# The opening of a retention and two-MLP kernel: a load moved by one place, the state's products ahead of y, and a first in-projection in three passes

## The chip, the cores and the metric

The kernel runs on one core of a Trainium2 chip. The metric is the device time of one execution in microseconds (us). Before the change it is 607.47 us, the median of three runs. One further execution was profiled; all rows below come from its trace.

## The reference

Three stages follow one another on 1,536 tokens (2 batches of 768) with 512 features.

```python
# 1. retention, 8 heads of 64, state carried along the 768 positions of a batch
state = gamma * state + outer(k[t], v[t])
y[t]  = scale * q[t] @ state
# 2. MLP, 512 -> 2048 -> 512
h = x @ w_in
x = (h * sigmoid(1.702 * h)) @ w_out
# 3. RMS norm, then a gated MLP, 512 -> 1536 -> 512
xn  = x / sqrt(mean(x * x) + 1e-6) * rms_g
out = (silu(xn @ w_gate) * (xn @ w_val)) @ w_out2
```

The weights of both MLPs come as float64. The kernel turns them into float32 itself.

## The kernel before

**Retention in chunks.** The sequence is cut into chunks of 128 positions, 6 to a batch. For chunk c the kernel loads two tiles of 512 KB: qk (queries and keys, `load_qk`) and kv (keys and values with positions on the partitions, `load_kv`). GpSimd scales them to qd and kd (`prep`, L225 and L232). TensorE forms the scores (`score_products`, L252), VectorE multiplies them by the decay masks (`masks`, L264), and TensorE sums y in PSUM from two parts: `inter` (L281: the state of the chunk before, times qd) and `intra` (L294: masked scores times values). `update_products` (L333: kd times values) gives the chunk's addition to the state. ScalarE decays the old state (`decay`, L341), VectorE adds (`add_update`, L349). y becomes x, split in two float32r tiles that sum to it: ScalarE writes the high part (`x_high`, L310), VectorE the low part (`x_low`, L316).

**Weights.** `load_next` (L138) loads one half of a weight block, 512 KB of float64, into one of 4 buffers; `queue` sets their order: first half of block 0, first half of block 1, second half of block 0, and so on. `convert_next` makes it float32: two ScalarE operations (L165, L166), then three of VectorE (`convert_rest`, L171, L172, L174). With `split=True` it issues the two of ScalarE and returns the rest, to be issued later. Without it, it also issues one more load at the end. A converted half is then split again into float32r high and low tiles (`split_in` for the first MLP's input weights, tiles wih and wil; `split_out` for its output weights, woh and wol): ScalarE L369, VectorE L370.

**First MLP.** A block of 512 tokens (4 chunks) goes through 128 hidden features at a time, a step. `in_proj` sums 12 products in one PSUM bank: for each of 4 slices of the 512 features, high by high, high by low and low by high (L364 to L366). Then ScalarE's gelu (L396) and its high part gh (L398), VectorE's low part gl (L399), and 12 products per step that accumulate the output (acc).

**Order.** The code around the change is the opening: chunks 0 to 3, which make up the first token block, the first conversions, and `prep(4)`. Its order on TensorE, VectorE, ScalarE and GpSimd is the order in which it is written, since `in_order` chains each instruction to the one before on its engine. Loads go through one queue of SP in the order written. After the opening a planner orders the work by the order of the code and by when it expects inputs to be ready; the first two steps are held behind the last instruction of the opening on each engine. Step 0 issues two conversions, the splits for its output and for step 2's input, then its in-projection and gelu; the accumulation of step 0 is issued in step 1, with the decay and state of chunk 4.

Of the kernel before, what the change touches and what calls it, by code (L numbers as in the profile page):

```python
# [23 lines left out]
KD = DM // 128  # L24
# [25 lines left out]
def tile_retention_mlp_swiglu(  # L50
# [19 lines left out]
    nc = tc.nc  # L70
# [12 lines left out]
    ps_t = pool("ps_t", 2, space=PSUM)  # L83
# [20 lines left out]
    def psum(p, name):  # L104
        return p.tile([128, T], F32, tag=p.name, name=name)
# [27 lines left out]
    def load_next():  # L133
        n = count["loaded"]
        if n < len(queue):
            kind, i, half = queue[n]
            t = st_p.tile([128, 512], U64, tag="st", name=f"{kind}{i}{half}_64")
            nc.sync.dma_start(out=t, in_=sources[kind][i][:, half * 512:half * 512 + 512])  # L138
            words[queue[n]] = t
            count["loaded"] += 1  # L140

    def convert_next(split=False):
        n = count["converted"]
        if n < len(queue):
            rest = convert(*queue[n])
            count["converted"] += 1
            if split:
                return rest
            rest()
            load_next()  # L150

    def convert(kind, i, half):

        if kind == "w1" and half == 0:
            raw[kind, i] = wr_p.tile([128, 1024], U32, tag="wr", name=f"{kind}{i}")  # L160
        o = slice(half * 512, half * 512 + 512)
        w = words.pop((kind, i, half)).bitcast(U32).rearrange("p (n two) -> p n two", two=2)
        low, high = w[:, :, 0], w[:, :, 1]
        q, t = tmp(f"q{kind}{i}{half}"), tmp(f"u{kind}{i}{half}").bitcast(U32)
        nc.scalar.activation(out=q, in_=high.bitcast(F32), func=ACTF.Copy, scale=2.0 ** -112)  # L165
        nc.scalar.activation(out=t, in_=low, func=ACTF.Copy, scale=2.0 ** -29)  # L166
        m = q.bitcast(U32)
        return lambda: convert_rest(kind, i, half, o, high, q, m, t)
# [17 lines left out]
    parts = {}  # L186
# [20 lines left out]
    xt = {}  # L207

    def load_qk(c):
        p, tag = (wr_p, "wr") if c < CPB else (ld_p, "ld")  # L210
        t = p.tile([128, 2, NP, C], F32, tag=tag, name=f"qk{c}")
        nc.sync.dma_start(out=t.rearrange("p a n c -> p (a n c)"), in_=qk[c])
        ld["qk", c] = t

    def load_kv(c):
        p, tag = (wr_p, "wr") if c < CPB else (ld_p, "ld")
        t = p.tile([128, 2, H, D], F32, tag=tag, name=f"kv{c}")
        nc.sync.dma_start(out=t.rearrange("p a h d -> p (a h d)"), in_=kv[c])
        ld["kv", c] = t
# [3 lines left out]
    def prep_q(c):  # L223
        t = tmp(f"qd{c}")
        nc.gpsimd.tensor_tensor(  # L225
            out=t.rearrange("p (n c) -> p n c", n=NP), in0=ld["qk", c][:, 0], in1=qd_sb, op=ALU.mult
        )
        at["qd", c] = t

    def prep_k(c):  # L230
        t = tmp(f"kd{c}")
        nc.gpsimd.tensor_tensor(  # L232
            out=t.rearrange("p (h d) -> p h d", h=H),
            in0=ld["kv", c][:, 0],
            in1=sm_sb[:, 0:H].to_broadcast([128, H, D]),
            op=ALU.mult,
        )
        at["kd", c] = t

    def prep(c):  # L240

        if c % NC:
            prep_q(c)
        if c % NC < NC - 1:
            prep_k(c)

    def score_products(c, p):
        t = ld["qk", c]
        sc = at["sc", c] = [psum(p, f"sc{c}_{e}") for e in range(2)]
        for n in range(NP):  # L250
            for e in range(2):
                nc.tensor.matmul(  # L252
                    out=sc[e][:, n * C:(n + 1) * C],
                    lhsT=t[64 * e:64 * e + 64, 1, n, :],
                    rhs=t[64 * e:64 * e + 64, 0, n, :],
                    start=True,
                    stop=True,
                )
# [14 lines left out]
    def inter(c, p):  # L273
        y = at["y", c] = psum(p, f"y{c}")
        if c % NC == 0:
            return
        qd = at.pop(("qd", c))
        for n in range(NP):
            for e in range(2):
                r = slice(64 * e, 64 * e + 64)  # L280
                nc.tensor.matmul(  # L281
                    out=y[r, n * C:(n + 1) * C],
                    lhsT=S_two[(c - 1) % 2][r, n, :],
                    rhs=qd[r, n * C:(n + 1) * C],
                    start=(n == 0),
                    stop=False,
                    skip_group_check=True,
                )

    def intra(c):  # L290
        y = at["y", c]
        for n in range(NP):
            for e in range(2):
                nc.tensor.matmul(  # L294
                    out=y[64 * e:64 * e + 64, n * C:(n + 1) * C],
                    lhsT=ld["kv", c][:, 1, 2 * n + e, :],
                    rhs=at["a", c, e][:, n * C:(n + 1) * C],
                    start=(c % NC == 0 and n == 0),
                    stop=True,
                    skip_group_check=True,  # L300
                )

    def x_of(c):
        j, i = divmod(c, CPB)
        if j not in xt:
            xt[j] = [xt_p.tile([128, KD, T], F32R, tag=f"xt{min(j, 1)}{s}", name=f"xt{j}{s}") for s in "hl"]
        return [x[:, :, i * C:(i + 1) * C] for x in xt[j]]

    def x_high(c):
        nc.scalar.activation(  # L310
            out=x_of(c)[0], in_=at["y", c].rearrange("p (n c) -> p n c", n=NP), func=ACTF.Copy
        )

    def x_low(c):
        xh, xl = x_of(c)
        nc.vector.tensor_tensor(  # L316
            out=xl, in0=at.pop(("y", c)).rearrange("p (n c) -> p n c", n=NP), in1=xh.bitcast(F32), op=ALU.subtract
        )
# [7 lines left out]
    def update_products(c, p):  # L326
        u = at["u", c] = psum(p, f"u{c}")
        kd = at.pop(("kd", c))
        vt = ld["kv", c][:, 1].rearrange("p h d -> p (h d)")
        for n in range(NP):  # L330
            for e in range(2):
                h = slice((2 * n + e) * D, (2 * n + e) * D + D)
                nc.tensor.matmul(  # L333
                    out=u[64 * e:64 * e + 64, n * D:(n + 1) * D], lhsT=kd[:, h], rhs=vt[:, h], start=True, stop=True
                )

    def decay(c):
        if c % NC:
            S_old, S_sb = S_two[(c - 1) % 2], S_two[c % 2]
            for n in range(NP):  # L340
                nc.scalar.activation(  # L341
                    out=S_sb[:, n, :], in_=S_old[:, n, :], func=ACTF.Copy, scale=sm_sb[:, H + n, :]
                )

    def add_update(c):
        u3 = at.pop(("u", c))[:, 0:NP * D].rearrange("p (n d) -> p n d", n=NP)
        S_sb = S_two[c % 2]
        if c % NC:
            nc.vector.tensor_tensor(out=S_sb, in0=u3, in1=S_sb, op=ALU.add)  # L349
        else:  # L350
            nc.vector.tensor_copy(out=S_sb, in_=u3)
# [9 lines left out]
    def product(out, a, b, first, last):  # L361

        (ah, al), (bh, bl) = a, b
        nc.tensor.matmul(out=out, lhsT=ah, rhs=bh, start=first, stop=False)  # L364
        nc.tensor.matmul(out=out, lhsT=ah, rhs=bl, start=False, stop=False)  # L365
        nc.tensor.matmul(out=out, lhsT=al, rhs=bh, start=False, stop=last)  # L366
# [10 lines left out]
        halves(hi, lo, g)  # L377
        return hi, lo

    def in_proj(ps, w, x):  # L380
        for k in range(KD):
            product(ps, [t[:, k * 128:(k + 1) * 128] for t in w], [t[:, k, :] for t in x], k == 0, k == KD - 1)


    gt = {}
# [2 lines left out]
    def mlp1_in(i):  # L388
        j, f, _, _ = STEPS[i]
        ps = psum(ps_h, f"h{j}_{f}")  # L390
        in_proj(ps, parts.pop(("wi", i)), xt[j])
        return ps

    def mlp1_act(i, ps):
# [347 lines left out]
    nc.sync.dma_start(out=qd_sb.rearrange("p n c -> p (n c)"), in_=qdec)  # L742
    load_kv(1)
    load_qk(2)
    load_next()
    load_kv(2)
    load_qk(3)
    load_kv(3)
    for _ in range(3):
# [26 lines left out]
    x_high(1)  # L776
    add_update(1)
    x_low(1)
    rest = convert_next(split=True)
    decay(2)  # L780

    score_products(2, ps_a)
    masks(2)
    inter(2, ps_h)
    score_products(3, ps_a)
    rest()
    intra(2)
    update_products(2, ps_t)
    prep(3)
    masks(3)  # L790
    x_high(2)
    add_update(2)
    x_low(2)
    split_in(0)
    rest = convert_next(split=True)
    decay(3)
    inter(3, ps_h)
    intra(3)
    update_products(3, ps_t)
    rest()  # L800
    x_high(3)
    x_low(3)
    add_update(3)
    load_next()
    load_next()
    split_in(1)
    prep(4)
    ends = in_order(opening)
# [16 lines left out]
    for i, (j, f, first, last) in enumerate(STEPS):  # L825
# [5 lines left out]
        k = min(i, len(STEPS) - 5)  # L831
# [5 lines left out]
        ps = mlp1_in(i)  # L837
# [76 lines left out]
    for g in range(0, F2, 2):  # L914
# [7 lines left out]
        n = len(work) - 10  # L922
# [31 lines left out]
    for g in range(0, JOIN, 2):  # L954
        reload("w2", g)
        reload("w2", g + 1)
        w = [set_tasks(k, g) for k in ("wg", "wv")]
# [96 lines left out]
```

## Time and profile before

| | us |
|---|---|
| median of 3 runs | 607.47 (606.02 to 608.62) |
| profiled execution: device time | 605.8 |
| profiled execution: span of the trace | 604.0 |
| TensorE matmul busy | 591.9 (98%) |
| VectorE busy | 443.1 (73%) |
| ScalarE busy | 365.0 (60%) |
| GpSimd busy | 28.1 (5%) |

The span is that of the trace; the device time holds a little more. A matmul's busy time overlaps that of the next, because matmuls are pipelined; so TensorE's share says that it seldom waits, not that it is at its peak. The granted TensorE clock is full in all 40 slices of the span.

### The profile page before, as it was taken

To read this page: it belongs to the slowest core of one execution; us is meant where nothing else is said; L and a number is where in the kernel's file an instruction comes from. 1 tells how busy PE (TensorE), PEld (TensorE's weight loads), DVE (VectorE), ACT (ScalarE), POOL (GpSimd) and SP (SyncE) were. 2 spreads that over 40 slices of the span, in tenths; PEclk is the share of its full clock that TensorE was granted. 3 is DMA by queue.
4 is the path that set the end of the run, shared out by engine and by line. 5 is a ranking of instruction groups with operands and counts; after the bars stand their busy time and mean duration, and the time that the engine had idled before them with its cause. 6 is when DMAs were issued, how large, how long until landed. Compare 5 with 4: busy or idle time off the path is not lost.

```text
span 604.0 us, 9246 instructions
## 1 busy us (share of the span) xinstructions
PE 591.9 (98%) x3354; PEld 492.8 (82%) x3354; DVE 443.1 (73%) x793; ACT 365.0 (60%) x691; POOL 28.1 (5%) x28
## 2 busy tenths in 40 slices
PE   7899999999999999999999999999999999999997
PEld 5677878888888878888887788898988889988885
DVE  3899988777797868989977999664655756655542
ACT  3577767766666658877757876453444536544532
POOL 3502200000112000000000000000000000000000
PEclk9999999999999999999999999999999999999999
DMA  8876744434678545337523423130221376643521
GB/s 337 343 232 239 245 157 139 126 122 144 187 220 244 160 139 163 105 95 235 159 105 97 128 107 124 69 112 30 98 77 65 110 247 219 228 144 105 174 71 69
DMA packets 32877, 93.14 MB, mean 154 GB/s; under 512 B 3904, under 2 KB 4160, under 8 KB 32832
## 3 DMA queue, kind: packets, MB, share of 16 engines
q1 hardware_dynamic: 32400, 92.42, 47.4%
q8 instruction: 26, 0.43, 0.3%
q10 hardware_dynamic: 432, 0.14, 0.1%
q14 instruction: 19, 0.16, 0.1%
HBM read 73.67 MB, written 18.87 MB: 153 GB/s over the span
## 4 chain that ended last, share of the span: by engine, by line
PE 85%; DVE 7%; DMA 3%; ACT 3%; issue 2%; ACTq 0%; SPq 0%; DVEq 0%
PE acc L364 6%; PE acc L365 6%; PE h L365 6%; PE acc L366 6%; PE h L364 6%; PE h L366 6%; PE o L364 5%; PE o L365 5%; PE o L366 5%; DMA qk<-in_qk 2%; DVE qw L172 1%; DVE wil L370 1%; DVE w L174 1%; DVE qw L171 1%; PE sc L252 1%
## 5 line engine op out<-in xcount | busy, mean ns | idle before, releaser
L364 PE MATMUL acc<-gh,woh 128*128 128x512 f32 x192 | 76.2, 399 | 0.9 <-ACT gh L398 0.9
L365 PE MATMUL acc<-gl,woh 128*128 128x512 f32 x192 | 75.2, 391 | 0.7 <-DVE gl L399 0.7
L366 PE MATMUL acc<-gh,wol 128*128 128x512 f32 x192 | 74.9, 390 | 0.0
L369 ACT ACTIVATE wih<-w 128x512 fp32r<-128x512 f32 x48 | 30.2, 631 | 53.5 <-PE h L365 51.5
L365 PE MATMUL o<-w3l,gh 128*128 128x512 f32 x144 | 56.3, 391 | 0.0
L364 PE MATMUL o<-w3h,gh 128*128 128x512 f32 x144 | 56.1, 391 | 0.0
L366 PE MATMUL o<-w3h,gl 128*128 128x512 f32 x144 | 56.1, 390 | 0.0
L370 DVE TENSOR_TENSOR wil<-w,wih 128x512 fp32r<-128x512 f32 x48 | 34.7, 726 | 22.3 <-ACT wih L369 22.2
L172 DVE CUSTOM_DVE_ANT_0 qw<-qw,uw 128x1024 uint16<-128x1024 uint16 x68 | 49.6, 730 | 0.8
L165 ACT ACTIVATE qw<-w 128x512 f32<-128x512 f32 x68 | 45.3, 666 | 1.0 <-DMA w<-in_w 1.0
L166 ACT ACTIVATE uw<-w 128x512 uint32<-128x512 uint32 x68 | 45.5, 670 | 0.0
L364 PEld LDWEIGHTS acc<-gh,woh 128*128 128x128 f32 x192 | 36.0, 188 | 9.7 <-ACT gh L398 1.2
L365 PEld LDWEIGHTS acc<-gl,woh 128*128 128x128 f32 x192 | 36.1, 188 | 8.5 <-DVE gl L399 1.6
L366 PEld LDWEIGHTS acc<-gh,wol 128*128 128x128 f32 x192 | 36.1, 188 | 7.5
L369 ACT ACTIVATE woh<-w 128x512 fp32r<-128x512 f32 x48 | 30.2, 630 | 16.6 <-DVE w L174 10.7
L171 DVE TENSOR_SCALAR qw<-qw 128x512 uint32<-128x512 uint32 x68 | 30.4, 448 | 10.5 <-ACT qw L165 10.5
L370 DVE TENSOR_TENSOR wol<-w,woh 128x512 fp32r<-128x512 f32 x48 | 32.9, 686 | 4.6 <-ACT woh L369 4.6
L370 DVE TENSOR_TENSOR gl<-gw,gh 128x512 fp32r<-128x512 f32 x24 | 16.6, 692 | 26.8 <-ACT gh L369 26.7
L399 DVE SCALAR_TENSOR_TENSOR gl<-g,gh 128x512 fp32r<-128x512 f32 x48 | 33.1, 689 | 3.1 <-ACT gh L398 1.4
L369 ACT ACTIVATE gh<-gw 128x512 fp32r<-128x512 f32 x24 | 15.1, 631 | 28.5 <-PE o L365 24.5
L366 PEld LDWEIGHTS o<-w3h,gl 128*128 128x128 f32 x144 | 27.0, 188 | 5.5
L364 PEld LDWEIGHTS o<-w3h,gh 128*128 128x128 f32 x144 | 27.1, 188 | 4.8 <-ACT w3h L369 0.2
(1115 smaller groups left out, 1509.1 us busy)
## 6 DMA issues: line engine op xcount, KB each, us to landing
w<-in_w SPq DMA_DIRECT2D x68, 512.0 KB, 4.7
qk<-in_qk SPq DMA_DIRECT2D x12, 512.0 KB, 6.8
kv<-in_kv SPq DMA_DIRECT2D x12, 512.0 KB, 6.7
g0d<-gs SPq DMA_DIRECT2D x12, 256.0 KB, 2.2
g2d<-gl SPq DMA_DIRECT2D x12, 256.0 KB, 2.1
gw<-g0d SPq DMA_DIRECT2D x12, 256.0 KB, 2.8
gw<-g2d SPq DMA_DIRECT2D x12, 256.0 KB, 2.7
out<-o SPq DMA_DIRECT2D x11, 256.0 KB, 2.4
```

Of the source, the lines that this page charges most:

```text
L165: nc.scalar.activation(out=q, in_=high.bitcast(F32), func=ACTF.Copy, scale=2.0 ** -112)
L166: nc.scalar.activation(out=t, in_=low, func=ACTF.Copy, scale=2.0 ** -29)
L171: nc.vector.tensor_scalar(out=m, in0=m, scalar1=3, scalar2=None, op0=ALU.logical_shift_left)
L172: nc.vector.tensor_tensor(out=m, in0=m, in1=t, op=ALU.add)
L174: nc.vector.scalar_tensor_tensor(out=dst, in0=high, scalar=0x80000000, in1=m, op0=ALU.bitwise_and, op1=ALU.bitwise_or)
L252: nc.tensor.matmul(out=sc[e][:, n * C:(n + 1) * C], lhsT=t[64 * e:64 * e + 64, 1, n, :], rhs=t[64 * e:64 * e + 64, 0, n, :], start=True, s ...
L364: nc.tensor.matmul(out=out, lhsT=ah, rhs=bh, start=first, stop=False)
L365: nc.tensor.matmul(out=out, lhsT=ah, rhs=bl, start=False, stop=False)
L366: nc.tensor.matmul(out=out, lhsT=al, rhs=bh, start=False, stop=last)
L369: nc.scalar.activation(out=hi, in_=src, func=ACTF.Copy)
L370: nc.vector.tensor_tensor(out=lo, in0=src, in1=hi.bitcast(F32), op=ALU.subtract)
L399: nc.vector.scalar_tensor_tensor(out=lo, in0=g, scalar=1.0 / GELU, in1=hi.bitcast(F32), op0=ALU.mult, op1=ALU.subtract)
```

## The change

In the opening, the load of the first weight half goes behind chunk 2's kv. For chunk 2, the update products and the state's addition come before intra and y's two parts, and the rest of the first conversion comes just ahead of x's low part; scores 3 and masks 3 come behind it all. The second conversion is no longer spread around chunk 3: it is issued whole, behind chunk 3's state, in place of one of two loads there (the conversion issues that load itself). The in-projection of step 0 sums its 12 products in another order: all four high by high, then all four high by low (of x), then all four low (of the weights) by high.

```diff
-    def in_proj(ps, w, x):
-        for k in range(KD):
-            product(ps, [t[:, k * 128:(k + 1) * 128] for t in w], [t[:, k, :] for t in x], k == 0, k == KD - 1)
+    def in_proj(ps, w, x, by_part):
+        order = [(k, n) for k in range(KD) for n in range(3)]
+        if by_part:
+            order.sort(key=lambda o: o[1])
+        for o in order:
+            k, n = o
+            a, b = ((0, 0), (0, 1), (1, 0))[n]
+            nc.tensor.matmul(
+                out=ps, lhsT=w[a][:, k * 128:(k + 1) * 128], rhs=x[b][:, k, :], start=o == order[0], stop=o == order[-1]
+            )
...
-        in_proj(ps, parts.pop(("wi", i)), xt[j])
+        in_proj(ps, parts.pop(("wi", i)), xt[j], i == 0)
...
     load_kv(1)
     load_qk(2)
+    load_kv(2)
     load_next()
-    load_kv(2)
     load_qk(3)
     load_kv(3)
...
     x_low(1)
-    rest = convert_next(split=True)
     decay(2)
 
     score_products(2, ps_a)
     masks(2)
     inter(2, ps_h)
+    rest = convert_next(split=True)
+    update_products(2, ps_t)
+    add_update(2)
+    intra(2)
+    prep(3)
+    rest()
+    x_high(2)
+    x_low(2)
     score_products(3, ps_a)
-    rest()
-    intra(2)
-    update_products(2, ps_t)
-    prep(3)
     masks(3)
-    x_high(2)
-    add_update(2)
-    x_low(2)
     split_in(0)
-    rest = convert_next(split=True)
     decay(3)
     inter(3, ps_h)
     intra(3)
     update_products(3, ps_t)
-    rest()
     x_high(3)
     x_low(3)
     add_update(3)
     load_next()
-    load_next()
+    convert_next()
     split_in(1)
     prep(4)
```

## Rows read from the trace of the kernel before

**Rows 1.** Sums by stretch: busy us of each engine, clock, DMA share, GB/s.

```profile
15.00:20.00 5.00, 3.27 (x60) 2.79 (x56) 3.92 (x7) 1.24 (x5) 3.54 (x3) 1.00 1.01 408
35.00:80.00 45.00, 44.77 (x310) 35.83 (x311) 44.78 (x76) 34.16 (x66) 6.87 (x5) 1.00 0.70 235
34.90:604.00 569.10, 563.93 (x3016) 471.75 (x3016) 421.86 (x758) 347.37 (x654) 14.73 (x10) 1.00 0.46 144
```

**Rows 2.** Order of time, TensorE: start us, us, engine, line, operation, count, idle time before.

```profile
14.53 1.09 PE L281 MATMUL y<-qd,S_sb 64*64 64x128 f32 x16
...
17.30 1.16 PE L252 MATMUL sc<-qk 64*128 64x128 f32 x16 [1.68 <-DMA qk<-in_qk]
...
19.32 0.64 PE L333 MATMUL u<-kv,kd 128*64 128x64 f32 x16
...
20.64 1.09 PE L281 MATMUL y<-qd,S_sb 64*64 64x128 f32 x16 [0.69 <-DVE S_sb L349]
...
21.66 1.09 PE L294 MATMUL y<-a,kv 128*64 128x128 f32 x16
...
23.48 0.49 PE L364 MATMUL h<-xt0h,wih 128*128 128x512 f32 x1 [0.26 <-ACT xt0h L310]
...
24.23 0.50 PE L365 MATMUL h<-xt0l,wih 128*128 128x512 f32 x1 [0.27 <-DVE xt0l L316]
...
26.63 0.39 PE L366 MATMUL h<-xt0h,wil 128*128 128x512 f32 x1
...
34.86 0.50 PE L364 MATMUL acc<-gh,woh 128*128 128x512 f32 x1 [0.88 <-ACT gh L398]
```

**Rows 3.** Order of time, VectorE.

```profile
15.83 0.42 DVE L171 TENSOR_SCALAR qw<-qw 128x512 uint32<-128x512 uint32 x1
...
16.40 0.69 DVE L172 CUSTOM_DVE_ANT_0 qw<-qw,uw 128x1024 uint16<-128x1024 uint16 x1
...
17.12 0.69 DVE L174 SCALAR_TENSOR_TENSOR w<-w,qw 128x512 uint32<-128x512 uint32 x1
...
18.46 1.29 DVE L264 TENSOR_TENSOR a<-sc,dm_sb 128x512 f32<-128x512 f32 x2 [0.65 <-PE sc L252]
...
20.07 0.42 DVE L349 TENSOR_TENSOR S_sb<-u,S_sb 128x256 f32<-128x256 f32 x1 [0.32 <-PE u L333]
...
24.43 1.12 DVE L370 TENSOR_TENSOR wil<-w,wih 128x512 fp32r<-128x512 f32 x1
...
26.87 1.56 DVE L172 CUSTOM_DVE_ANT_0 qw<-qw,uw 128x1024 uint16<-128x1024 uint16 x1
```

**Rows 4.** Order of time, GpSimd.

```profile
12.11 1.27 POOL L225 TENSOR_TENSOR qd<-qk,qd_sb 128x512 f32<-128x512 f32 x1 [0.23 <-DMA qk<-in_qk]
...
14.79 1.04 POOL L232 TENSOR_TENSOR kd<-kv,sm_sb 128x512 f32<-128x512 f32 x1 [1.41 <-DMA kv<-in_kv]
...
17.23 1.71 POOL L225 TENSOR_TENSOR qd<-qk,qd_sb 128x512 f32<-128x512 f32 x1 [1.40 <-DMA qk<-in_qk]
...
23.72 1.28 POOL L225 TENSOR_TENSOR qd<-qk,qd_sb 128x512 f32<-128x512 f32 x1 [3.78 <-DVE w L174]
...
25.00 1.44 POOL L232 TENSOR_TENSOR kd<-kv,sm_sb 128x512 f32<-128x512 f32 x1
...
26.41 1.46 POOL L225 TENSOR_TENSOR qd<-qk,qd_sb 128x512 f32<-128x512 f32 x1
```

**Rows 5.** Order of time, ScalarE.

```profile
23.61 0.63 ACT L369 ACTIVATE wih<-w 128x512 fp32r<-128x512 f32 x1 [0.19 <-DVE w L174]
...
24.61 1.07 ACT L341 ACTIVATE S_sb<-S_sb,sm_sb 128x64 f32<-128x64 f32 x4 [0.36 <-DVE S_sb L349]
...
25.58 0.65 ACT L165 ACTIVATE qw<-w 128x512 f32<-128x512 f32 x1
...
29.40 0.64 ACT L369 ACTIVATE woh<-w 128x512 fp32r<-128x512 f32 x1 [1.47 <-DVE w L174]
...
31.20 0.63 ACT L369 ACTIVATE wih<-w 128x512 fp32r<-128x512 f32 x1 [1.17 <-DVE w L174]
```

## The prediction

> **What bounds the kernel now.** I read the sums by stretch first, then the order of time of each engine. From 34.90 us to the end TensorE is busy 563.9 of 569.1 us, at full granted clock [rows 1]; the first accumulation, which opens that stretch at 34.86, has waited 0.88 us for ScalarE's gh [rows 2]. So the long rest runs at TensorE's pace, and the opening can change the total only by moving the start of that first accumulation (34.86 us), or by making a new stall behind it. Busy TensorE is not TensorE at its peak, but its matmuls follow one another with next to no wait, and that is all the argument needs.
>
> Before 34.86, three stalls of TensorE lie in the way of the first in-projection [rows 2]: scores 3 wait 1.68 us for chunk 3's queries and keys (they start at 17.30), the update products of chunk 2 run only at 19.32, and inter 3 then waits 0.69 us for the state they feed; the in-projection itself starts at 23.48 and stalls before its second product, until 24.23, for the low half of x.
>
> Last, the other engines of that stretch. The reader should see in VectorE's rows [rows 3] and GpSimd's [rows 4] which of them are longer than their like. A GpSimd qd takes 1.27 us at 12.11 but 1.71 at 17.23, where VectorE's L174 had begun at 17.12: about 0.44 lost. VectorE's wil at 24.43 takes 1.12, and L172 at 26.87 takes 1.56, against 0.69 for L172 at 16.40. Both end some 0.56 after a GpSimd qd ends (25.00 and 27.87). The masks at 18.46 (1.29 for two) overlap GpSimd work without being longer. So an operation that reads two operands in SBUF (L172, L174, and the subtraction of a weight half, L370) and a GpSimd product shut each other out; masks, x-low and the state's addition, which read PSUM, don't.
>
> **Part 1: the two loads change places.** Both are 512 KB. DMA moves 408 GB/s here [rows 1], so one takes 0.524 MB / 408 = 1.28 us. Chunk 2's kd starts at 14.79, waiting on its keys and values, 2.68 us (two transfers) behind qd 2 at 12.11 [rows 4]. Swapped, it starts when qd 2 ends and one transfer has landed: 13.45, done 14.5. The weight half lands about 1.3 later, near 14.7. Everything behind the pair keeps its place in SP's queue, so chunk 3's data is there at 17.2 as before. Cost: none in itself. Even if decay 2 (1.07) and the half's two activations (0.65 each [rows 5]) all came behind its landing, they would end at 17.1, before L172 wants them at 17.2 (part 2).
>
> **Part 2: update products ahead of y.** Inter 2 starts at 14.53 and the next group may follow 1.02 later (as 20.64 to 21.66 [rows 2]): update products 15.55 to 16.2, state 2 by 16.7 (0.11 to the addition, 0.42 for it [rows 2, 3]), against 20.5. Intra 2 then ends at 17.2, before scores 3 can start. So 1.5 us of TensorE work (intra 2 and update) moves into its wait for chunk 3's data, and the 0.69 stall is gone. If nothing else were late, inter 3 would start at 18.6, and the opening gain 2 us.
>
> **What is late next.** VectorE does the state's addition at 16.3, then the weight half: L171 16.65, L172 17.2, L174 17.9 (spacings 0.57 and 0.72 from 15.83, 16.40, 17.12 [rows 3]), then x-low 2, then masks 3. GpSimd's qd 3 wants to start at 17.23. They meet. With L172 first, qd 3 runs from 17.75 to 19.0, and L174 waits behind it and ends 0.56 later, at 19.55. X-low (about 0.6, half of the masks' pair) and masks 3 (1.29) end at 21.45. Intra 3 starts at 21.5, against 21.66. The gain left of 2 us is 0.15. VectorE was idle there before; now masks 3 and all of TensorE behind them queue on that conversion.
>
> The Trainium skill, "SBUF — State Buffer", section "Who interferes with whom", says that a VectorE instruction with two SBUF inputs contends with a GpSimd instruction that reads SBUF, and that issue order decides which one blocks. The trace agrees: 1.71 for 1.27, and 1.56 for 0.69. With that rule the sum is the one below, +1.35; were the two merely sharing, it would be the first rival, -0.95.
>
> **Part 3: the first in-projection by parts.** The stall of about 0.5 between 23.48 and 24.23 goes, since four products of the high halves come first. It starts 1.82 behind intra 3 as before, at 23.3; eleven spacings of 0.24 ((26.63 - 24.23)/10) put its last product at 25.95, not 26.63 [rows 2]. TensorE is 0.7 ahead there, if it can use it. Twelve matmuls either way; no weight load is added.
>
> **Part 4: the second half's conversion is moved** behind x-high 3 and x-low 3. Its two activations fitted beside chunk 3 before; now they start at x-high 3's end. Intra 3 (1.09) ends at 22.6, x-high 3 at 23.2 and the two activations by 24.5. VectorE does x-low 3 at 23.25, state 3 at 23.8, L171 at 24.15, L172 at 24.7. GpSimd meanwhile does qd 4 to 25.0 and kd 4 [rows 4], if they start as now (below). L172 is held to 25.0 and ends 25.55, which holds kd 4 to 25.4, done 26.45 (as now). L174 waits for that and ends at 27.0. The weight's high half, which waits for it, was started at 23.61 [rows 5]; now at 27.05, 3.4 later. Wil, held by qd 5 in the same way (26.9 to 28.2), ends at 28.7, against 25.55. The bare instructions are the same as before: 3 of VectorE, 2 and 1 of ScalarE. The two loads issued at the opening's end stay two; one now waits for the second conversion's L174, as it did before through its buffer; I cost it at nothing, since neither half is converted before the first step's two.
>
> **Who waits for that.** In-projection 1 needs wil, so it ends near 31 as before and eats TensorE's 0.7. The conversions of the first step are held behind the opening on each engine. Before, their first L172 was held by qd 5 to 27.87 and ended 28.43; from 27.87 to the accumulation at 34.86 it is 6.99 us of L172, L171, L174, the next half, the activation table and gh. Now, from wil's end, L171 starts at 28.65 and L172 at 29.2, with GpSimd idle. That is 29.2 - 27.87 = +1.35 at the head of the chain that ends in the first accumulation; I let the 6.99 stand. Another 0.65 is lost if decay 4 (1.07) stays ahead of the first activation, as at 24.61 and 25.58 [rows 5]: L171 at 29.35, +2.0. I leave decay 4 behind, because the activations come first in the code (decay 4 belongs to the second step), and keep +2.0 as the forecast's upper end. The other end that I can't read is what qd 4 waits for: its row names an L174 [rows 4], through a buffer that the pool may give otherwise after the change. If it still waits for the second conversion, L174 ends at 26.1 unheld, qd 4 runs 26.25 to 27.5, wil ends at 28.05, kd 4 at 28.95, the first step's L172 at 29.5, and qd 5 (to 30.65) holds its L174 to 31.2, which by the spacings of rows 3 would have ended at 29.35 before: +1.85, within the same end.
>
> **The sum.** 604.0 + 1.35 = 605.35 of span. The profiled run took 605.8, so 1.8 lies outside: 607.15. The median of the three runs is 607.47, 1.67 above the profiled run: 608.8. VectorE, nearly always busy from 35 to 80 [rows 1], moves by the same 1.35 as TensorE, so I add no stall there. No term here reaches 0.5% (3.04 us), which is about what a measurement of this kernel can tell from no change.
>
> **The rivals.** (a) *The early start is kept.* Were the port met less (qd 3 and L172 miss one another), the weight half is done at 18.6, masks 3 at 20.4, intra 3 starts at 20.5, the second conversion ends near 25.1 and the first step's L172 runs at 26.9: 0.95 ahead, 606.5. If the first gelu is also placed ahead of the next half's weights, only TensorE sets the accumulation, and it gives at most its 1.7 at the last product of in-projection 0 plus the 0.88 wait: -2.6, 604.9. For it: the stalls taken away are real. Against it: the start times meet within 0.05 us. (b) *Nothing arrives at 34.86.* The first step holds 1.47 and 1.17 us in which ScalarE waits for L174 [rows 5], and the later conversion may fit there: 607.5. (c) *Slower than the bound.* GpSimd's qd 3 takes the port first, at 17.23. L172 ends at 19.05 and holds kd 3 until 18.95; L174 waits to 20.0, ends 20.55; masks 3 end at 22.4, intra 3 starts 0.75 later than now. The second conversion then meets qd 5 as well (L174 to 28.35), and the first step's L172 runs at 30.2: +2.35, 609.8; with decay 4 ahead, +3.0, 610.5. It decides from the point where qd 3 starts before about 17.2, or the state's addition ends after 16.7.
>
> **How the numbers follow.** The forecast (+0.5 to +2.0, 608.0 to 609.5) gets 0.45: its steps have rows. (a) 0.20, its far end rarely; (b) 0.20; (c) 0.15, half of it beyond 0.5%. Faster by over 0.5% would need more than all of (a): 0.03. Slower by over 0.5%: half of (c) and a little of the forecast: 0.10. Within: 0.87. The range reaches from 605.4, which leaves out the far end of (a) (0.05), to 610.2, which leaves out that of (c) (0.10).
>
> **What would show it.** Right: update products 2 near 15.6, scores 3 near 17.3, L174 of the first half 1.2 us or longer, masks 3 ending after 21, the first in-projection unbroken, the second wih near 27, the first accumulation near 36 after a wait of about 2. Wrong: L174 at its plain 0.69 and masks 3 ending at 20.4 (then (a)); the accumulation at 34.9 (then (b)); or a step order after the opening that puts other work ahead of the first gelu. A new wait behind 36 us would break the sum at its last step.

## The result, and the profile after

The changed kernel takes 610.04 us (median of 6 runs, 609.29 to 611.13) against 606.76 (605.25 to 608.62) for the kernel before, measured beside it: a ratio of 1.0054, 95% interval 1.0034 to 1.0075, or +3.28 us. The time lies inside the predicted range (605.4 to 610.2), the rise does not: counted from the 607.47 that it was added to, the range ended at +2.7. That the time still fell inside is luck: the kernel before measured 0.71 lower over six runs than over the first three. The rise is also just over the 0.5% that the prediction took for the least that can be measured, to which it had given a chance of 0.10. The forecast was a rise of 1.35 us; 1.9 us of the rise need another cause. The profiled execution took 610.54, with a span of 608.6. The mean granted clock of the six executions is 0.992 (two), 0.994 (three) and 0.997 of full; the profiled one is at 0.992, so the low clock weighs more in its trace than in the median.

Chunk 2's queries and keys landed some 0.5 us later than in the profile of before (inter 2 starts at 15.05, against 14.53 in [rows 2]). That differs from one execution to the next; I subtract it below as the loads' 0.5. Chunk 3's landed earlier instead (qd 3 at 16.63, against 17.23 in [rows 4]).

TensorE of the changed kernel in order of time, with the columns of [rows 2]:

```profile
15.05 1.09 PE L281 MATMUL y<-qd,S_sb 64*64 64x128 f32 x16
16.07 0.69 PE L333 MATMUL u<-kv,kd 128*64 128x64 f32 x16
...
17.56 1.16 PE L252 MATMUL sc<-qk 64*128 64x128 f32 x16
18.65 1.09 PE L281 MATMUL y<-qd,S_sb 64*64 64x128 f32 x16
21.72 0.44 PE L294 MATMUL y<-a,kv 128*64 128x128 f32 x2 [1.98 <-DVE a L264]
22.32 1.76 PE L294 MATMUL y<-a,kv 128*64 128x128 f32 x13 [0.16 <-DVE a L264]
...
25.07 1.34 PE L387 MATMUL h<-xt0h,wih 128*128 128x512 f32 x4
26.25 1.07 PE L387 MATMUL h<-xt0l,wih 128*128 128x512 f32 x4
27.16 1.07 PE L387 MATMUL h<-xt0h,wil 128*128 128x512 f32 x4
...
33.46 1.09 PE L281 MATMUL y<-qd,S_sb 64*64 64x128 f32 x16 [1.01 <-DVE a L264]
34.48 0.43 PE L294 MATMUL y<-a,kv 128*64 128x128 f32 x2
36.54 0.80 PE L387 MATMUL h<-xt0h,wih 128*128 128x512 f32 x1 [1.62 <-ACT g L403]
37.27 1.76 PE L294 MATMUL y<-a,kv 128*64 128x128 f32 x13
...
40.02 0.80 PE L364 MATMUL acc<-gh,woh 128*128 128x512 f32 x1
...
42.64 0.39 PE L364 MATMUL acc<-gh,woh 128*128 128x512 f32 x1
```

The update products of chunk 2 (16.07) run ahead of y, scores 3 no longer wait, and the first in-projection (25.07 to 28.2) is unbroken. But intra 3 stands 1.98 us behind masks 3. The row to stop at is 36.54: one single product of an in-projection in the middle of intra 4, behind a wait for a gelu, and behind it everything takes nearly twice its time (1.76 for 13 products of L294, against 1.09 for 16 at 21.66 in [rows 2]). It is the first product of in-projection 2. The two banks of its pool hold the results of in-projections 0 and 1, so it can start only when gelu 0 has read the first. The planner put it there; in the program of before it stood behind all 12 products of the first accumulation.

Busy time by stretch (columns: TensorE, its weight loads, VectorE, ScalarE, GpSimd, then granted clock, DMA share, GB/s), as [rows 1]:

```profile
21.72:25.90 4.18, 4.02 (x35) 3.57 (x36) 2.09 (x5) 1.94 (x5) 2.11 (x2) 0.59 1.03 409
...
36.50:42.50 6.00, 5.96 (x37) 4.93 (x38) 5.33 (x11) 5.99 (x12) 0.00 (x0) 0.50 0.62 213
...
40.02:608.60 568.58, 564.25 (x3016) 472.61 (x3015) 420.28 (x754) 345.44 (x650) 14.74 (x10) 1.00 0.45 143
```

Behind both waits the granted clock is low: 0.59 on average behind the one of chunk 3, and 0.50 (1.2 GHz, of 2.4) for 6 us behind that for the gelu. From the first accumulation to the end it is 568.6 us, against 569.1 [rows 1]: what was lost was lost by 40.02, where 34.86 stood before. The profiled executions differ by 4.6 us of span, the medians by 3.28, because that of before was 0.96 below its median and that of after 0.50 above.

VectorE, as [rows 3], and GpSimd, as [rows 4]:

```profile
17.20 0.98 DVE L171 TENSOR_SCALAR qw<-qw 128x512 uint32<-128x512 uint32 x1
18.33 0.69 DVE L172 CUSTOM_DVE_ANT_0 qw<-qw,uw 128x1024 uint16<-128x1024 uint16 x1
19.06 1.41 DVE L174 SCALAR_TENSOR_TENSOR w<-w,qw 128x512 uint32<-128x512 uint32 x1
...
20.99 1.27 DVE L264 TENSOR_TENSOR a<-sc,dm_sb 128x512 f32<-128x512 f32 x2
...
26.52 0.69 DVE L172 CUSTOM_DVE_ANT_0 qw<-qw,uw 128x1024 uint16<-128x1024 uint16 x1
27.25 0.69 DVE L174 SCALAR_TENSOR_TENSOR w<-w,qw 128x512 uint32<-128x512 uint32 x1
...
30.48 0.69 DVE L172 CUSTOM_DVE_ANT_0 qw<-qw,uw 128x1024 uint16<-128x1024 uint16 x1
```

```profile
16.63 1.27 POOL L225 TENSOR_TENSOR qd<-qk,qd_sb 128x512 f32<-128x512 f32 x1 [1.69 <-DMA qk<-in_qk]
18.57 1.35 POOL L232 TENSOR_TENSOR kd<-kv,sm_sb 128x512 f32<-128x512 f32 x1 [0.67 <-DMA kv<-in_kv]
23.68 1.27 POOL L225 TENSOR_TENSOR qd<-qk,qd_sb 128x512 f32<-128x512 f32 x1 [3.76 <-DMA qk<-in_qk]
25.06 1.04 POOL L232 TENSOR_TENSOR kd<-kv,sm_sb 128x512 f32<-128x512 f32 x1
```

Qd 3 (16.63 to 17.90) holds L171, kd 3 (18.57 to 19.92) holds L174, and masks 3 queue behind both. The first step's L172 runs at 30.48. ScalarE, of the changed kernel and then of the kernel before:

```profile
24.33 0.60 ACT L310 ACTIVATE xt0h<-y 128x512 fp32r<-128x512 f32 x1 [2.24 <-PE y L294]
...
27.97 0.63 ACT L369 ACTIVATE wih<-w 128x512 fp32r<-128x512 f32 x1 [1.93 <-DVE w L174]
28.51 0.81 ACT L341 ACTIVATE S_sb<-S_sb,sm_sb 128x64 f32<-128x64 f32 x3
29.23 0.66 ACT L165 ACTIVATE qw<-w 128x512 f32<-128x512 f32 x1
...
34.60 1.28 ACT L403 ACT_TABLE_LOAD   x1
35.89 0.60 ACT L403 ACTIVATE g<-h 128x512 f32<-128x512 f32 x1
```

```profile
31.85 1.28 ACT L396 ACT_TABLE_LOAD   x1
33.14 0.60 ACT L396 ACTIVATE g<-h 128x512 f32<-128x512 f32 x1
```

Gelu 0 is 2.75 later (2.25 without the loads' 0.5). From gelu to accumulation it is 4.13 us, against 1.72 before. So two separate losses stand in the profile: a late gelu, and 2.4 us more between it and the accumulation.

### The profile page after: what moved, and what is told of

It reads as the page before. It is cut to its first block, busy times and chain, and to the rows that moved or that the text cites. A ratio compares the mean times of both kernels' runs of the same rounds, so it can differ in the third digit from the quotient of the medians.

```text
span 608.6 us, 9246 instructions
## 1 busy us (share of the span) xinstructions
PE 597.5 (98%) x3354; PEld 497.5 (82%) x3354; DVE 444.5 (73%) x793; ACT 365.6 (60%) x691; POOL 27.4 (5%) x28
## 4 chain that ended last, share of the span: by engine, by line
PE 94%; ACT 2%; DVE 2%; DMA 1%; issue 1%; SPq 0%; POOL 0%; DVEq 0%; POOLq 0%
PE h L387 21%; PE acc L364 8%; PE acc L365 7%; PE acc L366 7%; PE o L365 5%; PE o L364 5%; PE o L366 5%; PE y L294 2%; PE y L281 2%; PE sc L252 1%; DMA qd_sb<-in_qdec 1%; PE v2a L660 1%; PE g10a L660 1%; PE g8a L660 1%; PE g6a L660 1%; PE v10a L660 1%
## 5 line engine op out<-in xcount | busy, mean ns | idle before, releaser
L172 DVE CUSTOM_DVE_ANT_0 qw<-qw,uw 128x1024 uint16<-128x1024 uint16 x68 | 48.7, 718 | 0.8
L165 ACT ACTIVATE qw<-w 128x512 f32<-128x512 f32 x68 | 45.2, 665 | 0.0
L171 DVE TENSOR_SCALAR qw<-qw 128x512 uint32<-128x512 uint32 x68 | 30.4, 448 | 10.3 <-ACT qw L165 10.2
```

Of the source, the lines that this page charges most:

```text
L171: nc.vector.tensor_scalar(out=m, in0=m, scalar1=3, scalar2=None, op0=ALU.logical_shift_left)
L172: nc.vector.tensor_tensor(out=m, in0=m, in1=t, op=ALU.add)
```

## The experiments

Ratios are against the kernel before, measured beside each group of experiments (its medians 606.47 to 606.67). A difference between two kernels that were not measured side by side is a difference of two ratios, each good to some 0.15% (that of the changed kernel to 0.2%); so such a difference is good to some 1.5 us.

**1. The planner's order restored.** The changed kernel, with step 2's first TensorE instruction tied behind step 1's last.

```diff
             mlp1_out(i - 1)
+            if i <= 2:
+                pe = [x for x in nc.cur_bb.bb.instructions[begun:] if x.engine == ENGINES[0]]
+                if i == 2:
+                    after(pe[0], ends["step1"])
+                ends["step1"] = pe[-1]
```

> The changed kernel, with the first product of in-projection 2 held behind step 1 on TensorE (in the changed kernel the planner put it between the second and third product of intra 4, where it waits 1.62 us for gelu 0). Theory A (the order drawn up by the planner costs most: TensorE waits, its clock falls to 0.50 from 35.8 to 42.4, and intra 4, the update and the first accumulation run at half speed): intra 4 and update 4 are done before gelu 0, the first accumulation starts near 37.6 instead of 40.0, and the time falls by 2 to 2.5 us, to about 0.1 to 0.2% above the kernel before. Theory B (only the conversions of weights are late, in front of gelu 0): the first accumulation waits for gh anyway, at the cost of the same low clock, and the time falls by less than 1 us.

608.12 us, ratio 1.0024 (1.0010 to 1.0038). TensorE with the row of gelu 0, and the clock by stretch:

```profile
33.80 1.09 PE L281 MATMUL y<-qd,S_sb 64*64 64x128 f32 x16 [0.84 <-DVE a L264]
...
36.23 0.60 ACT L403 ACTIVATE g<-h 128x512 f32<-128x512 f32 x1
...
36.34 0.72 PE L333 MATMUL u<-kv,kd 128*64 128x64 f32 x14
37.94 0.74 PE L364 MATMUL acc<-gh,woh 128*128 128x512 f32 x2 [0.88 <-ACT gh L405]
```

```profile
32.50:38.00 5.50, 3.52 (x52) 2.58 (x50) 4.06 (x8) 4.30 (x7) 0.00 (x0) 1.00 0.62 188
38.00:43.00 5.00, 5.00 (x21) 3.84 (x22) 5.00 (x10) 5.00 (x10) 0.00 (x0) 1.00 0.58 202
```

Intra 4 and update 4 are done before gh is, the wait for it is the 0.88 of before [rows 2], and the clock stays at 2.4 GHz. 0.30 points, about 1.8 us (0.3 to 3.3 by the two intervals), of the loss are gone, a little under theory A's 2 to 2.5: they belong to that one product's place and what it brings. What stays, +1.46 (0.6 to 2.3), is the size of the step that had been predicted.

**2. Masks 3 first.** The changed kernel, with scores 3 and masks 3 ahead of the rest of the first conversion.

```diff
-    rest()
     x_high(2)
-    x_low(2)
     score_products(3, ps_a)
     masks(3)
+    rest()
+    x_low(2)
```

> The changed kernel, with scores 3 and masks 3 in front of the rest of the first conversion and x-low 2. Theory A (VectorE's queue: masks 3 stand behind the conversion): intra 3 starts near 19.9 instead of 21.7 to 22.3, TensorE's 1.98 us wait and the stretch at 0.50 clock from 22 to 25.8 go, but the first conversion then ends about 1.3 later, so the first in-projection starts near 22 to 23 instead of 25.1; the time falls by 1 to 2.5 us. Theory B (what sets the first accumulation is gelu 0 alone, behind the conversions): the in-projection starts earlier but the first accumulation stays within 0.7 us of where it was, and so does the time.

609.53 us, ratio 1.0047 (1.0031 to 1.0063). Intra 3 now runs at 19.73 without a wait, but the wait only moves to the in-projection, and the later one stays:

```profile
24.14 1.20 PE L387 MATMUL h<-xt0h,wih 128*128 128x512 f32 x4 [2.44 <-ACT xt0h L310]
...
36.10 0.59 PE L387 MATMUL h<-xt0h,wih 128*128 128x512 f32 x1 [1.62 <-ACT g L403]
```

The in-projection starts 0.9 us earlier than after the change (inter 3 at 18.70 and 18.65), the gelu 0.44 (35.45), and the time is less by 0.07 points, 0.4 us, which the intervals don't tell from nothing. The 0.47% (0.31 to 0.63) that stays has no such wait, so intra 3's 1.98 us are not what makes the loss.

**3. The second conversion put back.** The changed kernel, with the second conversion around chunk 3 as before.

```diff
     split_in(0)
+    rest = convert_next(split=True)
     decay(3)
...
     update_products(3, ps_t)
+    rest()
...
     load_next()
-    convert_next()
+    load_next()
```

> The changed kernel, with the second conversion spread around chunk 3 as in the kernel before. Theory A (gelu 0 is late because the second conversion and what is behind it on ScalarE and VectorE are late): the second wih starts near 25 to 26 instead of 28.0, gelu 0 comes 1.5 to 2.5 us earlier, and the time falls by about as much. Theory B (TensorE's waits and its low clock in chunk 3 set the start of the in-projections, and the conversions are hidden behind them): gelu 0 moves by less than 0.7 us and the time stays within 1 us.

606.70 us, ratio 1.0002 (0.9988 to 1.0015). The whole loss is gone, nearest to theory A, and more than the gelu's lead of 1.34 us (34.55, against 35.89), although intra 3 still waits 2.11 and the clock is 0.57 from 22 to 26. The product of in-projection 2 still sits inside intra 4:

```profile
34.55 0.60 ACT L403 ACTIVATE g<-h 128x512 f32<-128x512 f32 x1
...
35.20 0.50 PE L387 MATMUL h<-xt0h,wih 128*128 128x512 f32 x1 [1.11 <-ACT g L403]
...
37.12 0.50 PE L364 MATMUL acc<-gh,woh 128*128 128x512 f32 x1
...
38.58 0.39 PE L364 MATMUL acc<-gh,woh 128*128 128x512 f32 x1
```

But its wait is 1.11, and none stands before inter 4; the clock stays at 2.4 GHz. The same instructions, from that product to the start of the seventh of the accumulation, take 3.38 us here and 6.10 after the change (36.54 to 42.64).

**4. The three passes alone.** The kernel before, with the new `in_proj` and nothing else of the diff.

> The kernel before with nothing but the in-projection of step 0 ordered by its three parts. It also makes the planner place the first product of in-projection 2 inside intra 4, as in the changed kernel, but with gelu 0 where it was (33.1). Theory A (that place is a fault by itself): intra 4 waits from about 32.5 for gelu 0 (33.8), the first accumulation comes about 1 us later than 34.86 in spite of 0.5 us saved at the in-projection, more if the clock falls; the time is 0.5 to 2 us above the kernel before. Theory B (the three passes bring their 0.5 us): 0.3 to 0.6 us below the kernel before.

607.16 us, ratio 0.9999 (0.9986 to 1.0013), between the two theories. Three passes alone make the planner pull in-projection 2's product into intra 4 (it runs at 35.03, after 1.08 for the gelu); with the second conversion in its old place that costs nothing that the interval of 0.85 us to either side shows. Nor does the new in-projection show a gain (it still waits 0.52 for the low half of x here). Its chunks 2 and 3 are in the order of before, and yet GpSimd and VectorE meet there:

```profile
16.85 1.26 POOL L225 TENSOR_TENSOR qd<-qk,qd_sb 128x512 f32<-128x512 f32 x1 [0.23 <-DMA qk<-in_qk]
...
17.05 1.61 DVE L172 CUSTOM_DVE_ANT_0 qw<-qw,uw 128x1024 uint16<-128x1024 uint16 x1
```

**5. The late second conversion alone.** The kernel before, with the second conversion whole behind chunk 3.

```diff
     split_in(0)
-    rest = convert_next(split=True)
     decay(3)
...
     update_products(3, ps_t)
-    rest()
...
     load_next()
-    load_next()
+    convert_next()
```

> The kernel before with nothing but the second conversion moved behind chunk 3's state, whole. The planner then also places the first product of in-projection 2 inside intra 4. Theory A (the late second conversion is the cause of the loss, through gelu 0 and the low clock behind TensorE's wait for it): the second wih starts 2 to 3 us later than 23.6, gelu 0 comes 1.5 to 2.5 us later than 33.1, the time is 1.5 to 3.5 us above the kernel before. Theory B (it needs the reordered chunk 2 beside it): less than 0.7 us above.

608.98 us, ratio 1.0041 (1.0027 to 1.0055). This part alone makes three quarters of the loss (by the intervals, it may be all of it), and the same picture:

```profile
34.58 1.09 PE L281 MATMUL y<-qd,S_sb 64*64 64x128 f32 x16 [0.64 <-DVE a L264]
...
37.66 0.50 PE L364 MATMUL h<-xt0h,wih 128*128 128x512 f32 x1 [1.63 <-ACT g L396]
```

The clock is 0.71 from 38 to 40 and 0.50 from 40 to 42. (This profiled execution was 2.4 us above the median, its opening late; its starts can't be compared with those of others, its waits can.)

**6. The wait filled.** The changed kernel, with 8 products on constants ahead of inter 4, and the rest of intra 4 tied behind in-projection 2's product so that this keeps its place. What is computed is the same. Update 4 slips ahead of that product here.

```diff
         ps = mlp1_in(i)
+        if i == 1:
+            warm = psum(ps_a, "warm4")
+            warming(8)
...
         next_of(att)
...
+            y4 = [x for x in nc.cur_bb.bb.instructions[n:] if x.engine == ENGINES[0]]
+        if i == 2:
+            after(y4[9], [x for x in nc.cur_bb.bb.instructions[begun:] if x.engine == ENGINES[0]][0])
         mlp1_act(i, ps)
```

> The changed kernel with 8 extra products that feed nothing, in front of inter 4 (1.7 us of TensorE work at full clock, in place of the waits at 32.5 and 34.9), the first product of in-projection 2 still held inside intra 4, where it waits for gelu 0; update 4 runs ahead of that product. Theory A (the clock: 6 us of work at 0.50 behind the wait cost 2.7 us): the granted clock stays at 1.00 from 33 to 43, the first accumulation starts near 38 instead of 40.0, the time falls by 2 to 3 us though gelu 0 is no earlier. Theory B (the wait itself, and what else is late, is the cost): the time falls by less than 0.8 us.

608.50 us, ratio 1.0035 (1.0023 to 1.0047): some 1.2 us less than the changed kernel, between the two theories, and by the intervals (-0.3 to 2.6) not told from nothing. The clock is 1.00 from 34 to 42, and the accumulation starts at 38.26. Since update 4 moved too, this is not the clock's price alone.

**7. The gelu's table loaded early.** The kernel before, with one more activation of one element at the start, of the function that the gelu uses, written where nothing reads it.

```diff
     warming(WARM)
+    nc.scalar.activation(out=pad[:, 0:1], in_=mean_w, func=ACTF.Silu)
     make_identity(nc, ident)
```

> The kernel before with a one-element gelu among ScalarE's first instructions, so that the activation table of gelu is loaded at the start, not in front of gelu 0 (1.28 us at 31.85). Theory A (gelu 0's chain on ScalarE sets the first accumulation): gelu 0 1.3 us earlier, the first accumulation 0.7 to 0.9 us earlier (update 4 ends at 34.0), the time 0.5 to 1 us below the kernel before. Theory B (something else is as late): within 0.3 us.

604.61 us, ratio 0.9974 (0.9956 to 0.9991): faster than both kernels, and by more than theory A had it. ScalarE loads the table at 0.73, and not at 31.85. Its rows ahead of the accumulation:

```profile
31.39 0.63 ACT L369 ACTIVATE wih<-w 128x512 fp32r<-128x512 f32 x1 [1.17 <-DVE w L174]
31.92 0.58 ACT L396 ACTIVATE g<-h 128x512 f32<-128x512 f32 x1
```

**8. The same line in the changed kernel.**

> The changed kernel with the same early table. Theory A (the wait for gelu 0 costs twice, once as a wait and once by the clock): TensorE's wait of 1.62 us shrinks to under 0.5, the clock does not fall behind it, and the time falls by 2.5 to 4 us, to the level of the kernel before or just under it. Theory B (gelu 0's time counts once): 1 to 1.5 us. Theory C (the first accumulation is held by something else): under 0.5 us.

606.15 us, ratio 0.9995 (0.9984 to 1.0007). One table load of 1.28 us taken off the chain takes 0.59 points off, about 3.6 us (2.2 to 5.0): as much as the loss. But the kernel before gains from the same line, and against experiment 7 the change still costs 0.21 points, about 1.3 us (0 to 2.5), about what it costs in experiment 1. TensorE and its clock:

```profile
33.77 1.09 PE L281 MATMUL y<-qd,S_sb 64*64 64x128 f32 x16 [1.02 <-DVE a L264]
...
35.42 0.50 PE L387 MATMUL h<-xt0h,wih 128*128 128x512 f32 x1 [0.20 <-ACT g L403]
```

```profile
38.00:42.00 4.00, 4.00 (x20) 3.30 (x19) 4.00 (x9) 4.00 (x9) 0.00 (x0) 1.00 0.80 263
```

The wait before inter 4 is the same (1.02), that for the gelu 0.20 and not 1.62, and the clock doesn't fall.

**9. Chunk 3's wait filled.** The changed kernel, with 8 products on constants between inter 3 and intra 3.

```diff
     inter(3, ps_h)
+    warm = psum(ps_t, "warm3")
+    warming(8)
     intra(3)
```

> The changed kernel with 8 extra products that feed nothing between inter 3 and intra 3 (1.7 us of TensorE work in place of its wait of 1.98 us for masks 3). Theory A (the clock of chunk 3 is part of the loss, since x-high 3, the second conversion and with it gelu 0 stand behind intra 3): the clock stays at 1.00 from 22 to 26, intra 3 takes 1.1 instead of 1.8 us, gelu 0 comes 0.7 to 1.0 us earlier, the time falls by 0.7 to 1.5 us. Theory B (TensorE's pace in chunk 3 is hidden behind the conversions): less than 0.4 us.

609.81 us, ratio 1.0052 (1.0040 to 1.0064): not to be told from the changed kernel. The clock is 1.00 from 22 to 26, but in-projection 1 then waits 0.52 for wil, and the product inside intra 4 again waits 1.62, with the clock at 0.50 from 38 to 40. The gelu does come earlier in this profile, at 35.43 (0.9 without the loads' differences), as theory A had it; the time doesn't show it. So chunk 3's low clock makes the gelu late, but taking it away alone brings no gain that is measured here.

**10. The rest of the change.** The changed kernel with the edits of 1, 3 and 7.

> The changed kernel with the second conversion spread as before, in-projection 2 held behind step 1 and gelu's table loaded early: what is left of the change is the load's place, the reordered chunk 2 and the three passes. Against the kernel before with the early table alone (0.9974 of the time before). Theory A (masks 3 behind the first conversion cost by themselves): TensorE still waits 2 us and runs at 0.50 in chunk 3, gelu 0 is 0.5 to 1.4 us later than there, and the time is 0.5 to 1.5 us more than that of the early table alone. Theory B (with the late conversion and the planner's order out of the way the state's early start is kept): equal or faster.

605.42 us, ratio 0.9973 (0.9962 to 0.9983): as 7 alone. So the swap of the loads, the update ahead of y and the three passes together cost or gain nothing that can be told here (some 1.2 us either way). The trace is theory A's: TensorE waits 2.10 us for masks 3, the clock is 0.58 from 22 to 26, and the gelu comes 1.26 later than in 7 (33.18 and 31.92). The time is theory B's.

**11. That, with masks 3 first.** The edits of 10 and 2 together.

> As the run with the rest of the change, and with scores 3 and masks 3 ahead of the first conversion's rest. Theory A (what counts is when the conversions end, not when TensorE starts): the wait moves from masks 3 to the first in-projection, gelu 0 within 0.5 us of the run with the rest of the change, and so the time. Theory B (the early state is worth its 2 us once masks 3 are first): 1 to 2 us below it, under the kernel before with the early table.

606.58 us, ratio 1.0012 (0.9994 to 1.0029). Half of scores 4 was planned ahead of the in-projection and waits there:

```profile
23.68 1.45 PE L252 MATMUL sc<-qk 64*128 64x128 f32 x8 [2.33 <-DMA qk<-in_qk]
```

The gelu is within 0.2 us of that of 10 (32.98 and 33.18). Taking chunk 3's wait away moved another instruction into it. The gelu is as theory A had it, the time is not: 0.39 points, 1.2 us by the medians, above 10, measured side by side. Of that the profiles show 0.43 at the first accumulation (35.78 and 35.35); the rest is not explained.

**12. Three passes and the early table.** The kernel before with the edits of 4, 1 and 7.

> The kernel before with the three passes, in-projection 2 held behind step 1 and gelu's table loaded early. Theory A (update 4 and gelu 0 set the first accumulation, and the 0.5 us saved at the in-projection are hidden behind the conversions): within 0.3 us of the early table alone. Theory B (the in-projection's start counts): 0.4 to 0.6 us below it.

605.19 us, ratio 0.9967 (0.9947 to 0.9986): not to be told from 7 or 10. The version to keep is 7, the kernel before with one line more.

## Why the prediction was right, and where it fell short

The forecast's direction held, and its path to the gelu in outline; two of its steps came out right in number by another way than forecast, and its sum lacked a term.

**Part 1 and Part 2: right up to the state.** Kd 2 (13.89; predicted 13.45, and 0.5 for the loads) and update products 2 (16.07; 15.55 and 0.5) came where they were expected. "Chunk 3's data is there at 17.2 as before" did not hold: qd 3 ran at 16.63. "What is late next" held in its outcome: the first half's conversion in front of masks 3 ended late beside GpSimd, and masks 3 at 22.26 (21.45 and 0.5). Its detail was off, and went as rival (c) begins: L172 did not come first and push qd 3 back; qd 3 held L171 at 0.98 instead of 0.42. I had reckoned only operations with two SBUF operands as held, and L171 has one. The Trainium skill, "SBUF — State Buffer", section "Who interferes with whom", lists tensor_scalar among the operations that can take the shared ports; the trace agrees, with this 0.98.

Nor is that meeting the change's alone. The rows of before are those of one execution, in which none of the first half's three operations was held. In experiments 4, 5, 7 and 12, where chunks 2 and 3 are in the order of before, at least one was: L172 took 1.61 in 4 and 1.63 in 5, L171 0.88 in 7, L174 1.64 in 12. The landing of chunk 3's queries, which sets when they meet, moved from one execution to the next (qd 3 at 15.90 in 7, 17.34 in 12). So the profile of before was not a typical one to forecast from, which fits its time, 0.96 below its median.

**Part 3: shape right, lead not.** The in-projection is unbroken, but it starts at 25.07 (predicted 23.3, and 0.5), since intra 3 ran at 0.59 of the clock. So TensorE was never 0.7 ahead; experiment 4 shows no gain either.

**Part 4 and "Who waits for that": right on the far end, in part by luck.** Wih of the second half starts at 27.97 (27.05 and 0.5), but not by the forecast steps. X-high 3 ends at 24.93, 1.2 later than 23.2 and 0.5, behind the slow intra 3. L172 and L174 were to be held by qd 4 and kd 4; by the time L172 ran, at 26.52, GpSimd was done with both (26.10), and they took their plain 0.69. The two misses cancel. Qd 4 is not tied to L174 but to its load (23.68). Wil then met qd 5 as forecast (1.20 at 28.64). Decay 4 came mostly ahead of the first step's activations (three of its four at 28.51, L165 at 29.23), which I had kept as the far end, +2.0 instead of +1.35. The first step's L172 at 30.48 stands 2.1 behind 27.87 without the loads' 0.5. From there to the gelu it is 5.41 us, and 5.27 before: the chain moved as a whole. With the order of before (experiment 1) the time rises by 1.46 us, less than 2.1; counted from inter 2's start, gelu 0 comes at 18.61 before and 20.84 after, but at 19.58 and 19.39 in experiments 3 and 4, whose times are those of before. Experiments 3 and 5 show that this part is what costs: undone, the loss is gone; alone, it gives +0.41%.

**The sum: the step that failed.** "I let the 6.99 stand", and with it "VectorE moves by the same 1.35 as TensorE, so I add no stall there". The 6.99 us held to the gelu but not from the gelu to the accumulation, where 1.72 became 4.13. Two assumptions of mine were in it. One, that the planner keeps TensorE's order behind an opening whose edits don't touch it. It does not: three passes alone or the late conversion alone are enough to put in-projection 2's product inside intra 4. So intra 4 and update 4, which had filled the time up to the gelu, stood behind it. The other, that the clock stays at 2.4 GHz, since in the profile of before it does so everywhere; behind 1.01 and 1.62 us of waiting it did not. (In other executions of the kernel before it does not either: of the 35 measured beside experiments 1 to 4, 9 have a mean clock of 0.994 to 0.997, and a median of 607.7 us, against 606.3 of the other 26.) I had named "a step order after the opening that puts other work ahead" as something that would prove me wrong, but gave it no price. The measured price is some 1.8 us (0.3 to 3.3; after against experiment 1).

How the 1.8 us divide between the product's place and the clock is bounded only. At full clock, with the product inside intra 4, gelu to accumulation takes 2.57 us in experiment 3, 2.56 in 4 and 2.55 in 8, against 1.72 before and 1.71 in 1: the place puts 0.85 there by itself. The rest of the 4.13, 1.56, came with the low clock. Over the same instructions up to the seventh of the accumulation experiment 3 is 2.7 us shorter without a wait among them, so that is what the low clock took there; not all of it can have reached the end, since the whole price is 1.8. Filling the wait (6) gives back 1.2 us, not told from nothing, with update 4 moved as well. Single executions with a mean clock of 0.999 to 1.000 and the product inside intra 4 took 608.13 (5) and 609.24 (9), those of experiment 1 at 1.000 took 607.36 to 608.19; they don't settle it. Experiments 3 and 4 have the place without a measured loss (0.85 lies at the edge of their intervals): it took a late gelu as well, and the two together gave a longer wait and a low clock.

**The rivals.** (a) and (b) are out. Of (c), both signs were met: qd 3 took the port first, before 17.2, and the state's addition ended at 17.29 (16.8 without the loads' 0.5), after 16.7. The time came near its 609.8, but not by its steps: the second conversion did not meet qd 5 (28.02 to 29.29, with L174 done at 27.94).

Starts in single profiles carry the argument to some 1 to 2 us, not to tenths: from the first accumulation to the end it is 569.1 before, 568.6 after, 569.0 in experiment 1 and 567.3 in experiment 3. Why the planner moves the product stays open; the runs show only which edits do it.

## What to carry to other kernels

When an edit makes one engine's chain late, look at what a planner or an order has put behind the instruction that waits for it, and price that as well: here a late chain that costs 1.5 us with the old order cost 3.3, through one product whose place shows no loss while the chain is on time. A wait that was filled in the middle of the opening gained nothing measurable (experiment 9): the product behind the late gelu still waited 1.62 us. What helped was to shorten the chain that ends last, here the conversions and the gelu on VectorE and ScalarE: one activation of one element that loads a table ahead of time gained more than any reordering of TensorE's work did here. And read more than one execution before forecasting a meeting of two engines from starts that differ by tenths: in the first conversion, the profile of before showed none, and four others of that order did.

## What the hardware showed that I had not expected

A granted clock that falls behind one idle stretch of TensorE and not behind another of the same length:

| kernel | idle of TensorE | clock behind it |
|---|---|---|
| after | 1.98 (to 21.72) | 0.59 over 21.72 to 25.90 |
| after | 1.01, then 1.62 (to 36.54) | 0.50 over 36.5 to 42.5 |
| experiment 2 | 2.44 (to 24.14) | 1.00 over 24.14 to 26.00 |
| experiment 2 | 0.83, then 1.62 (to 36.10) | 0.59 over 36 to 38 |
| experiment 4 | 2.26 (to 21.82) | 1.00 over 22 to 26 |
| experiment 5 | 2.28 (to 22.01) | 0.50 over 22 to 24 |
| experiment 1 | 0.84, 0.26, then 0.88 (to 37.94) | 1.00 over 38 to 43 |
| experiment 3 | 1.11 (to 35.20) | 1.00 over 34 to 38 |

What tells 2.26 in experiment 4 from 2.28 in experiment 5 stays open. So for a wait of about 2 us, the low clock is a cost to be kept at one end of the range, and neither to be left out nor to be taken as sure.

Taking the table load of 1.28 us off the kernel before gained 1.6 us (0.5 to 2.7 by the interval), and off the changed kernel 3.6 (2.2 to 5.0): it seems that the price of a piece of the chain depends on what waits behind it.
